# Own buffers for the mirrored gates, and mirror work on 480 of 512 columns in two of three blocks

## The chip, the cores and the metric

The kernel runs on one core of a Trainium2 chip. The metric is the device time of one execution in microseconds (us), given as the median over several executions. The engines are called as in the profile: PE (TensorE matmuls) with PEld (its weight loads), DVE (VectorE), ACT (ScalarE), POOL (GpSimd) and SP (SyncE, which here only issues DMAs). A small q after an engine's name is its instruction queue.

## The reference

The input x has 8 batches of 3008 tokens with 256 features. First comes a Fourier mixing, of which the real part is kept, and then a gated feed-forward layer with 1536 hidden features:

```python
X = np.fft.fft(x, axis=1)
X = np.fft.fft(X, axis=2)
x = X.real.reshape(24064, 256)
gate = np.maximum(x @ w_gate, 0.0)
val = x @ w_val
out = gate * val @ w_out
```

## The kernel before, in words

**Symmetry.** Token k and token 3008 - k of a batch are mirrors: with the feature transform folded into the weights (tiles wc and ws for the cosine and sine parts), both come from the same two rows of numbers P and Q. A token's gate is wc·P + ws·Q, its mirror's is wc·P - ws·Q. The kernel computes the first, reads it, and then adds -2·ws·Q (weights wm) to the same PSUM bank to get the second. The same holds for the value.

**Blocks and steps.** Per batch b there are three blocks of 512 columns (blk 0, 1, 2). A column is a token with its mirror; each group of 32 columns holds the tokens ka + 94·kb of one ka (0 to 47) and all 32 kb. The mirrors of ka = 0 and of ka = 47 lie in the same group, so these two groups are their own mirrors: the first 32 columns of block 0 and the last 32 of block 2. The mirrored half of their results is computed and never stored (`store` leaves it out). Per block there are 12 slices f of 128 hidden features. One step t is one (b, blk, f), 288 in all, and a loop writes the instructions of every engine in the order in which they run (a manual schedule; each engine's queue is in order).

**One step** does the following, with the line numbers of the profile:
- `gate(t)`: two 512-column matmuls into PSUM tile G (L432, L433), and ACT writes the plain gate gs = Relu(G) (L434).
- `mirror_gate(t)`, at the start of step t + 1: one more matmul onto G (L439), and ACT writes the mirrored gate gm = Relu(G) (L442).
- `value(t, 0)`, `value(t, 1)`: two matmuls into V (L449, L451), then DVE writes the plain half of the hidden tile h = gs·V (L453).
- The mirrored value has two forms. A step with t >= 44 and t % 3 != 2 is a *split* step: DVE makes E from V between the two value matmuls (`even`, L459), later E = 2E - V (L473), and POOL multiplies gm·E into the mirrored half of h (`mirror_h`, L465 on POOL). Any other step uses a third value matmul on V (L476), and DVE multiplies gm·V (L465 on DVE).
- `out_piece`: 8 matmuls of 256 columns (L494) for the block 12 steps back, each reading 128 columns of one h tile. Every three steps ACT copies a finished PSUM tile to an output tile os (L497), every six SP issues its four stores (L506 or L512).

So three steps (t % 3 = 0, 1, 2) form a triple with two split steps and one other. In this text a triple runs from one L439 of a step with t % 3 = 0 to the next such one.

**Buffers.** gs and gm share five buffers (pool gp). E has three (ep), os three (op), h 25 (hp). G has two PSUM banks, V three. A buffer is handed on in the order in which its readers stand in the program. In the steady state gs of a step with t % 3 = 0 takes the buffer of gm of step t - 3, and a gs of a step with t % 3 = 1 that of gs of step t - 2.

**The next batch's input.** While batch b is worked on, batch b + 2 is loaded: SP loads xl (L82), POOL issues an indirect load xh (L85). Then POOL folds it (L99 to L108), 22 pieces put one after the other behind the steps' `mirror_h`, from step 13 of each batch for b >= 2 and from step 34 for b = 0 (two per step there). PE's stage 1 (L161, L166) reads the folded tile in the next batch; a shuffle through DRAM (L179, L185), `rotate` (L191) and stage 2 (L203) make the next P and Q. POOL thus has two duties: `mirror_h` for the current step and the fold of a later batch.

Of the kernel before, what the change touches and what calls it, by code (L numbers as in the profile page):

```python
# [11 lines left out]
F32 = mybir.dt.float32  # L12
BF16 = mybir.dt.bfloat16
I32 = mybir.dt.int32
ALU = mybir.AluOpType
ACTF = mybir.ActivationFunctionType
SB = bass.MemoryType.SB
# [9 lines left out]
def free(ap, offset, *dims):  # L27

    part = list(ap.ap[0])
    return bass.AP(ap.tensor, ap.offset + offset, [part] + [list(d) for d in dims])  # L30
# [12 lines left out]
def kernel(ctx: ExitStack, tc, x, w_gate, w_val, w_out, out):  # L43
# [3 lines left out]
    nc = tc.nc  # L47
    B, S, D = x.shape
    DF = w_gate.shape[1]
    NA, NB = 94, 32  # L50
# [3 lines left out]
    NBLK = 3  # L54
# [139 lines left out]
    pqt, nbt = {}, {}  # L194
# [33 lines left out]
    wm = [const.tile([128, DF], BF16, tag=f"wm{i}", name=f"wm{i}") for i in range(2)]  # L228
    wo = const.tile([128, NF, D], BF16, tag="wo")
    af = const.tile([128, NF], F32, tag="af")  # L230
# [38 lines left out]
    with tc.tile_pool(name="sp", bufs=1, space=SB) as sp:  # L269
# [103 lines left out]
        for cs in range(2):  # L373
            t2 = sp.tile([128, 4, NB], F32, tag=f"m2t{cs}")
            nc.vector.tensor_scalar(t2[:], kbi[:], scalar1=mul[:], scalar2=offs[cs][:],
                                    op0=ALU.mult, op1=ALU.add)
# [11 lines left out]
                                op0=ALU.is_equal, op1=ALU.mult)  # L388
# [23 lines left out]
    stage2(0, 0, 1, "dve")  # L412


    gp = ctx.enter_context(tc.tile_pool(name="gp", bufs=5, space=SB))
    ep = ctx.enter_context(tc.tile_pool(name="ep", bufs=3, space=SB))
    op = ctx.enter_context(tc.tile_pool(name="op", bufs=3, space=SB))

    steps = [(b, blk, f) for b in range(B) for blk in range(NBLK) for f in range(NF)]
    ht = {}  # L420

    def split(t):

        return NBLK * NF + 8 <= t < len(steps) and t % 3 != 2

    def gate(t):
        b, blk, f = steps[t]
        pq, fs = pqt[b, blk], slice(f * 128, (f + 1) * 128)
        e = ht[t] = {"h": hp.tile([128, 2, 512], BF16, tag="h", name="h"),
                     "G": psg.tile([128, 512], F32, tag="g", name="G"),  # L430
                     "gs": gp.tile([128, 512], F32, tag="gs", name="gs")}
        nc.tensor.matmul(e["G"][:], lhsT=wc[0][:, fs], rhs=pq[:, 0, :], start=True, stop=False)  # L432
        nc.tensor.matmul(e["G"][:], lhsT=ws[0][:, fs], rhs=pq[:, 1, :], start=False, stop=True)  # L433
        nc.scalar.activation(e["gs"][:], e["G"][:], ACTF.Relu)  # L434

    def mirror_gate(t):
        b, blk, f = steps[t]
        e = ht[t]
        nc.tensor.matmul(e["G"][:], lhsT=wm[0][:, f * 128:(f + 1) * 128], rhs=pqt[b, blk][:, 1, :],  # L439
                         start=False, stop=True, skip_group_check=True)  # L440
        e["gm"] = gp.tile([128, 512], F32, tag="gs", name="gm")
        nc.scalar.activation(e["gm"][:], e["G"][:], ACTF.Relu)  # L442

    def value(t, part):
        b, blk, f = steps[t]
# [8 lines left out]

    def even(t):
        b, blk, f = steps[t]
        e = ht[t]
        e["E"] = ep.tile([128, 512], F32, tag="e", name="E")
        nc.vector.scalar_tensor_tensor(e["E"][:], nbt[b, blk][:], af[:, f:f + 1], e["V"][:],  # L459
                                       op0=ALU.mult, op1=ALU.add)  # L460

    def mirror_h(t, eng, val):

        e = ht[t]
        eng.tensor_tensor(free(e["h"][:], 512 + NB - 1, [NB, 16], [-1, NB]),  # L465
                          e["gm"][:].rearrange("p (a k) -> p a k", k=NB),
                          val[:].rearrange("p (a k) -> p a k", k=NB), op=ALU.mult)

    def mirror_value(t):
        b, blk, f = steps[t]  # L470
        e = ht[t]
        if split(t):
            nc.vector.scalar_tensor_tensor(e["E"][:], e["E"][:], 2.0, e["V"][:], op0=ALU.mult, op1=ALU.subtract)  # L473
            mirror_h(t, nc.gpsimd, e["E"])
        else:
            nc.tensor.matmul(e["V"][:], lhsT=wm[1][:, f * 128:(f + 1) * 128], rhs=pqt[b, blk][:, 1, :],  # L476
                             start=False, stop=True, skip_group_check=True)
            mirror_h(t, nc.vector, e["V"])

# [67 lines left out]
    for t in range(n + NF):  # L547
        if 0 < t <= n:
            mirror_gate(t - 1)
        if t < n:  # L550
            gate(t)
        if 0 < t <= n:
            if split(t - 1):
                value(t - 1, 1)
            else:
                mirror_value(t - 1)
        if t < n and not split(t):
            value(t, 0)
            value(t, 1)
        for fn in extra.get(t, ()):  # L560
            fn()
        if t >= NF:
            out_piece(t - NF, 0)
        if split(t):
            value(t, 0)
            even(t)
        if t >= NF:
            out_piece(t - NF, 1)
        if 0 < t <= n and split(t - 1):
            mirror_value(t - 1)  # L570
        for k in range(2 if t < NBLK * NF + 8 else 1):
            while folds and next(folds[0], folds) is folds:
                folds.pop(0)
# [30 lines left out]
```

## Time and profile before

| | |
|---|---|
| median of 3 runs | 690.17 us (690.15 to 691.46) |
| the profiled execution | 690.58 us, its span 688.8 us |
| granted TensorE clock | 0.998 |
| busy share of the span | PE 95%, PEld 61%, DVE 74%, ACT 63%, POOL 62% |
| first and last gs | 36.6 us and 671.0 us from the span's start |

The profiled execution is 0.41 us above the median; 1.8 us of it lie outside the span. A row of a view of groups gives busy time, mean duration of one instruction in ns, and the idle time of the engine just before these instructions with what ended it. A row of the view of waits gives the waiting instruction, what it waited for, the total in us, the number of times and the longest. A row of the timeline gives start, duration, engine, line and tiles. Matmuls overlap in it: what a matmul costs is the distance to the next start, not its duration.

### The profile page before, as it was taken

The numbers are of one execution on the slowest core, as the hardware profiler recorded it, in microseconds if no ns is written. First come the engines' busy times: TensorE is split into PE (matmuls) and PEld (weight loads), VectorE is DVE, ScalarE is ACT, GpSimd is POOL, SyncE is SP. The second block draws the span as 40 slices with busy tenths as digits, with TensorE's granted clock in tenths as the row PEclk, the third lists the DMA queues.
The fourth block names the chain that finished last, engine by engine and source line by source line (L and its number), as shares of the span: only waits on it lengthen the run. The fifth ranks groups of instructions, "written<-read, shape, count | busy, mean of one in ns | idle before, by whom it ended". The sixth has DMA issues, their size and how long they took to land.

```text
span 688.8 us, 12467 instructions
## 1 busy us (share of the span) xinstructions
PE 653.0 (95%) x4297; PEld 419.5 (61%) x4297; DVE 508.5 (74%) x800; ACT 436.2 (63%) x811; POOL 424.1 (62%) x398
## 2 busy tenths in 40 slices
PE   2799999999999999999999999999899999999996
PEld 1444665666566656666666666666566666666665
DVE  8447555578778778787778878778788788888881
ACT  5555665667676766676666757676666856665561
POOL 1219801984998499747995399846996343344331
PEclk9999999999999999999999999999999999999999
DMA  9692257239314822176112931258211241211213
GB/s 235 216 218 37 63 143 173 48 97 203 113 50 122 199 79 74 40 167 203 38 42 67 234 105 41 74 124 216 59 48 38 60 123 38 78 32 36 54 31 90
DMA packets 31843, 70.74 MB, mean 103 GB/s; under 512 B 4410, under 2 KB 21426, under 8 KB 29394
## 3 DMA queue, kind: packets, MB, share of 16 engines
q1 hardware_dynamic: 29444, 58.16, 31.6%
q0 software_dynamic: 2336, 11.80, 8.4%
q8 instruction: 33, 0.54, 0.4%
q14 instruction: 30, 0.25, 0.1%
HBM read 39.77 MB, written 30.96 MB: 103 GB/s over the span
## 4 chain that ended last, share of the span: by engine, by line
PE 61%; POOL 18%; DMA 10%; issue 5%; DVE 2%; ACT 2%; SPq 1%; POOLq 0%; DVEq 0%
PE po L494 24%; PE V L451 7%; POOL h L465 7%; PE G L439 6%; PE G L432 6%; PE G L433 6%; PE V L449 6%; DMA xl<-in_x_dram 5%; POOL xl L100 4%; POOL xc L99 4%; PE V L476 3%; DMA xh<-in_x_dram,ix 3%; DMA xh<-in_x_dram 2%; PE psw L251 2%; POOL eo L101 2%
## 5 line engine op out<-in xcount | busy, mean ns | idle before, releaser
L494 PE MATMUL po<-wo,h 128*128 128x256 bf16 x2304 | 323.2, 272 | 0.0
L465 POOL TENSOR_TENSOR h<-gm,E 128x512 bf16<-128x512 f32 x162 | 205.9, 1271 | 166.6 <-DVE E L473 166.0
L494 PEld LDWEIGHTS <-h 128*128 128x128 bf16 x2304 | 222.8, 98 | 83.5 <-issue 7.5
L442 ACT ACTIVATE gm<-G 128x512 f32<-128x512 f32 x288 | 172.5, 599 | 129.8 <-PE G L439 128.2
L453 DVE TENSOR_TENSOR h<-gs,V 128x512 bf16<-128x512 f32 x288 | 190.7, 685 | 58.7 <-PE V L451 47.1
L434 ACT ACTIVATE gs<-G 128x512 f32<-128x512 f32 x288 | 171.6, 596 | 15.0 <-POOL h L465 12.6
L465 DVE TENSOR_TENSOR h<-gm,V 128x512 bf16<-128x512 f32 x126 | 86.7, 688 | 85.6 <-ACT gm L442 60.8
L459 DVE SCALAR_TENSOR_TENSOR E<-nb,af,V 128x512 f32<-128x512 bf16 x162 | 120.8, 746 | 6.6 <-PE V L449 6.1
L439 PE MATMUL G<-pq,wm_107 128*128 128x512 bf16 x288 | 109.1, 379 | 9.9 <-ACT gs L434 9.5
L473 DVE SCALAR_TENSOR_TENSOR E<-E,V 128x512 f32<-128x512 f32 x162 | 110.2, 680 | 0.0
L432 PE MATMUL G<-pq,wc_103 128*128 128x512 bf16 x288 | 109.1, 379 | 1.0 <-ACT pq L206 1.0
L449 PE MATMUL V<-pq,wc_104 128*128 128x512 bf16 x288 | 109.1, 379 | 0.0
L433 PE MATMUL G<-pq,ws_105 128*128 128x512 bf16 x288 | 109.1, 379 | 0.0
L451 PE MATMUL V<-pq,ws_106 128*128 128x512 bf16 x288 | 109.0, 379 | 0.0
L497 ACT COPY os<-po 128x512 f32<-128x512 f32 x96 | 56.2, 585 | 67.9 <-PE po L494 67.9
L99 POOL TENSOR_TENSOR xc<-xl,xh 94x768 f32<-94x768 f32 x35 | 63.4, 1811 | 50.0 <-DMA xl<-in_x_dram 34.1
L100 POOL TENSOR_TENSOR xl<-xl,xh 94x768 f32<-94x768 f32 x35 | 63.4, 1812 | 1.6
L433 PEld LDWEIGHTS <-ws_105 128*128 128x128 bf16 x288 | 28.1, 98 | 35.0 <-issue 1.1
L451 PEld LDWEIGHTS <-ws_106 128*128 128x128 bf16 x288 | 28.1, 98 | 34.2 <-DVE ws_106 L256 0.4
L476 PE MATMUL V<-pq,wm_108 128*128 128x512 bf16 x126 | 47.7, 379 | 0.3
L432 PEld LDWEIGHTS <-wc_103 128*128 128x128 bf16 x288 | 28.1, 98 | 18.6 <-issue 15.6
L449 PEld LDWEIGHTS <-wc_104 128*128 128x128 bf16 x288 | 28.2, 98 | 17.6 <-issue 1.3
(361 smaller groups left out, 385.5 us busy)
## 6 DMA issues: line engine op xcount, KB each, us to landing
out_dram<-os SPq DMA_DIRECT2D x176, 128.0 KB
xl<-in_x_dram SPq DMA_DIRECT2D x7, 1360.0 KB
nb<-Nd SPq DMA_DIRECT2D x24, 128.0 KB
xl<-in_x_dram SPq DMA_DIRECT2D x7, 238.0 KB
xl<-in_x_dram SPq DMA_DIRECT2D x2, 768.0 KB
xh<-in_x_dram SPq DMA_DIRECT2D x2, 768.0 KB
wst<-in_moe_w_gate_dram SPq DMA_DIRECT2D x6, 256.0 KB
wst<-in_moe_w_val_dram SPq DMA_DIRECT2D x6, 256.0 KB
```

The source lines that it names most:

```text
L432: nc.tensor.matmul(e["G"][:], lhsT=wc[0][:, fs], rhs=pq[:, 0, :], start=True, stop=False)
L433: nc.tensor.matmul(e["G"][:], lhsT=ws[0][:, fs], rhs=pq[:, 1, :], start=False, stop=True)
L434: nc.scalar.activation(e["gs"][:], e["G"][:], ACTF.Relu)
L439: nc.tensor.matmul(e["G"][:], lhsT=wm[0][:, f * 128:(f + 1) * 128], rhs=pqt[b, blk][:, 1, :], start=False, stop=True, skip_group_check=True)
L442: nc.scalar.activation(e["gm"][:], e["G"][:], ACTF.Relu)
L449: nc.tensor.matmul(e["V"][:], lhsT=wc[1][:, fs], rhs=pq[:, 0, :], start=True, stop=split(t))
L451: nc.tensor.matmul(e["V"][:], lhsT=ws[1][:, fs], rhs=pq[:, 1, :], start=False, stop=True, skip_group_check=split(t))
L453: nc.vector.tensor_tensor(e["h"][:, 0, :], e["gs"][:], e["V"][:], op=ALU.mult)
L459: nc.vector.scalar_tensor_tensor(e["E"][:], nbt[b, blk][:], af[:, f:f + 1], e["V"][:], op0=ALU.mult, op1=ALU.add)
L465: eng.tensor_tensor(free(e["h"][:], 512 + NB - 1, [NB, 16], [-1, NB]), e["gm"][:].rearrange("p (a k) -> p a k", k=NB), val[:].rearrange("p ...
L473: nc.vector.scalar_tensor_tensor(e["E"][:], e["E"][:], 2.0, e["V"][:], op0=ALU.mult, op1=ALU.subtract)
L494: nc.tensor.matmul(po[:, s % 2, :], lhsT=ht[t - f + ff]["h"][:, sg, g * 128:(g + 1) * 128], rhs=wo[:, ff, :], start=(ff == 0), stop=(ff == ...
```

## The change

Three things are changed.

1. gm leaves the pool it shared with gs and gets four buffers of its own, in ep beside E, which goes from three to four. gs keeps two buffers. os goes from three to two. The bytes used are the same. With its own four buffers in turn, gm of step t takes the buffer of gm of step t - 4, and gs that of gs of step t - 2.
2. In blocks 0 and 2 every operation on mirrored gates and values (L439, L442, L459, L465, L473, L476 of before) runs on the 480 columns that have a mirror elsewhere.
3. The 32 columns of h that are left out are set to zero by POOL in `gate` (new line L444), since `out_piece` still reads them. These are 192 memsets, one per step of blocks 0 and 2.

```diff
@@ -412,12 +412,17 @@
     stage2(0, 0, 1, "dve")
 
 
-    gp = ctx.enter_context(tc.tile_pool(name="gp", bufs=5, space=SB))
-    ep = ctx.enter_context(tc.tile_pool(name="ep", bufs=3, space=SB))
-    op = ctx.enter_context(tc.tile_pool(name="op", bufs=3, space=SB))
+    gp = ctx.enter_context(tc.tile_pool(name="gp", bufs=2, space=SB))
+    ep = ctx.enter_context(tc.tile_pool(name="ep", bufs=4, space=SB))
+    op = ctx.enter_context(tc.tile_pool(name="op", bufs=2, space=SB))
 
     steps = [(b, blk, f) for b in range(B) for blk in range(NBLK) for f in range(NF)]
     ht = {}
+
+    def mirrored(t):
+
+        blk = steps[t][1]
+        return slice(NB if blk == 0 else 0, 512 - NB if blk == NBLK - 1 else 512)
 
     def split(t):
 
@@ -432,14 +437,19 @@
         nc.tensor.matmul(e["G"][:], lhsT=wc[0][:, fs], rhs=pq[:, 0, :], start=True, stop=False)
         nc.tensor.matmul(e["G"][:], lhsT=ws[0][:, fs], rhs=pq[:, 1, :], start=False, stop=True)
         nc.scalar.activation(e["gs"][:], e["G"][:], ACTF.Relu)
+        cols = mirrored(t)
+        if cols.stop - cols.start < 512:
+
+            lo = 0 if cols.start else cols.stop
+            nc.gpsimd.memset(e["h"][:, 1, lo:lo + NB], 0.0)
 
     def mirror_gate(t):
         b, blk, f = steps[t]
-        e = ht[t]
-        nc.tensor.matmul(e["G"][:], lhsT=wm[0][:, f * 128:(f + 1) * 128], rhs=pqt[b, blk][:, 1, :],
+        e, cols = ht[t], mirrored(t)
+        nc.tensor.matmul(e["G"][:, cols], lhsT=wm[0][:, f * 128:(f + 1) * 128], rhs=pqt[b, blk][:, 1, cols],
                          start=False, stop=True, skip_group_check=True)
-        e["gm"] = gp.tile([128, 512], F32, tag="gs", name="gm")
-        nc.scalar.activation(e["gm"][:], e["G"][:], ACTF.Relu)
+        e["gm"] = ep.tile([128, 512], F32, tag="gm", name="gm")
+        nc.scalar.activation(e["gm"][:, cols], e["G"][:, cols], ACTF.Relu)
 
     def value(t, part):
         b, blk, f = steps[t]
@@ -454,26 +464,27 @@
 
     def even(t):
         b, blk, f = steps[t]
-        e = ht[t]
+        e, cols = ht[t], mirrored(t)
         e["E"] = ep.tile([128, 512], F32, tag="e", name="E")
-        nc.vector.scalar_tensor_tensor(e["E"][:], nbt[b, blk][:], af[:, f:f + 1], e["V"][:],
+        nc.vector.scalar_tensor_tensor(e["E"][:, cols], nbt[b, blk][:, cols], af[:, f:f + 1], e["V"][:, cols],
                                        op0=ALU.mult, op1=ALU.add)
 
     def mirror_h(t, eng, val):
 
-        e = ht[t]
-        eng.tensor_tensor(free(e["h"][:], 512 + NB - 1, [NB, 16], [-1, NB]),
-                          e["gm"][:].rearrange("p (a k) -> p a k", k=NB),
-                          val[:].rearrange("p (a k) -> p a k", k=NB), op=ALU.mult)
+        e, cols = ht[t], mirrored(t)
+        eng.tensor_tensor(free(e["h"][:], 512 + cols.start + NB - 1, [NB, (cols.stop - cols.start) // NB], [-1, NB]),
+                          e["gm"][:, cols].rearrange("p (a k) -> p a k", k=NB),
+                          val[:, cols].rearrange("p (a k) -> p a k", k=NB), op=ALU.mult)
 
     def mirror_value(t):
         b, blk, f = steps[t]
-        e = ht[t]
+        e, cols = ht[t], mirrored(t)
         if split(t):
-            nc.vector.scalar_tensor_tensor(e["E"][:], e["E"][:], 2.0, e["V"][:], op0=ALU.mult, op1=ALU.subtract)
+            nc.vector.scalar_tensor_tensor(e["E"][:, cols], e["E"][:, cols], 2.0, e["V"][:, cols],
+                                           op0=ALU.mult, op1=ALU.subtract)
             mirror_h(t, nc.gpsimd, e["E"])
         else:
-            nc.tensor.matmul(e["V"][:], lhsT=wm[1][:, f * 128:(f + 1) * 128], rhs=pqt[b, blk][:, 1, :],
+            nc.tensor.matmul(e["V"][:, cols], lhsT=wm[1][:, f * 128:(f + 1) * 128], rhs=pqt[b, blk][:, 1, cols],
                              start=False, stop=True, skip_group_check=True)
             mirror_h(t, nc.vector, e["V"])
```

The order of PE, ACT, DVE and SP is unchanged but for the sizes. POOL's is not. The first place is POOL's queue behind the fold of batch 1, ahead of the load xh for batch 2 (steps 0 to 36). Before:

```order
63 L108 TENSOR_TENSOR eo<-xl 94x2x127 x2
64 L85 DMA xh<-in_x_dram,ix 96x4096
65 L99 TENSOR_TENSOR xc<-xl,xh 94x768
66 L100 TENSOR_TENSOR xl<-xl,xh 94x768
67 L101 TENSOR_TENSOR eo<-xc 94x3x127
```

And with the change, at the same place:

```order
63 L108 TENSOR_TENSOR eo<-xl 94x2x127 x2
64 L444 MEMSET h 128x32 x17
65 L85 DMA xh<-in_x_dram,ix 96x4096
66 L444 MEMSET h 128x32 x6
67 L99 TENSOR_TENSOR xc<-xl,xh 94x768
68 L100 TENSOR_TENSOR xl<-xl,xh 94x768
69 L444 MEMSET h 128x32
70 L101 TENSOR_TENSOR eo<-xc 94x3x127
```

The load xh of batch 2 now stands behind 17 memsets, those of steps 0 to 11 and 24 to 28. The memset of step 28 writes the h buffer of step 3, which `out_piece` reads for the last time at the end of step 22.

The second place is POOL's queue in block 2 of a batch, where `mirror_h` and the fold of a later batch alternate (this piece is in batch 2). Before:

```order
157 L100 TENSOR_TENSOR xl<-xl,xh 94x768
158 L465 TENSOR_TENSOR h<-gm,E 128x16x32
159 L101 TENSOR_TENSOR eo<-xc 94x3x127
160 L103 CAST eo<-xl 94x6
161 L104 TENSOR_TENSOR eo<-xl 94x3x127
162 L465 TENSOR_TENSOR h<-gm,E 128x16x32
163 L99 TENSOR_TENSOR xc<-xl,xh 94x768
164 L465 TENSOR_TENSOR h<-gm,E 128x16x32
```

And with the change:

```order
200 L100 TENSOR_TENSOR xl<-xl,xh 94x768
201 L475 TENSOR_TENSOR h<-gm,E 128x16x32
202 L101 TENSOR_TENSOR eo<-xc 94x3x127
203 L444 MEMSET h 128x32
204 L103 CAST eo<-xl 94x6
205 L104 TENSOR_TENSOR eo<-xl 94x3x127
206 L444 MEMSET h 128x32
207 L475 TENSOR_TENSOR h<-gm,E 128x15x32
208 L99 TENSOR_TENSOR xc<-xl,xh 94x768
209 L444 MEMSET h 128x32
210 L475 TENSOR_TENSOR h<-gm,E 128x15x32
```

Each step of the block puts one memset between the pieces of the fold and the `mirror_h` of the step before, which is one group of 32 columns shorter.

## Prediction

> **What bounds the kernel now.** I read the page first: engine shares and the chain that ended last.
>
> ```profile
> PE 653.0 (95%) x4297; PEld 419.5 (61%) x4297; DVE 508.5 (74%) x800; ACT 436.2 (63%) x811; POOL 424.1 (62%) x398
> PE 61%; POOL 18%; DMA 10%; issue 5%; DVE 2%; ACT 2%; SPq 1%; POOLq 0%; DVEq 0%
> ```
>
> PE is nearly always busy, yet 18% of the chain is POOL, an engine idle 38% of the time: in some stretches POOL holds PE back. The view of waits says how.
>
> ```profile
> ACT gs L434 <- POOL h L465: 12.6, 16, 1.2
> PE G L439 <- ACT gs L434: 9.5, 14, 1.0
> ```
>
> gs takes the buffer in which the gm of three steps earlier lay; that is free when POOL's `mirror_h` has read it, and L439 may not add to G before gs has read G. Asked by stretch of time, the second wait falls nearly all in the four stretches in which POOL folds during batches 2 to 5, about 2.4 us in each; batches 6 and 7, with nothing left to fold, have none. One of them in the timeline (batch 3), with a product of DVE and the gs two steps later:
>
> ```profile
> 322.69 1.27 POOL L465 TENSOR_TENSOR h<-gm,E 128x512 bf16<-128x512 f32 x1
> 324.00 0.60 ACT L434 ACTIVATE gs<-G 128x512 f32<-128x512 f32 x1 [0.91 <-POOL h L465]
> 324.65 0.38 PE L439 MATMUL G<-pq,wm_107 128*128 128x512 bf16 x1 [0.72 <-ACT gs L434]
> 325.78 0.69 DVE L453 TENSOR_TENSOR h<-gs,V 128x512 bf16<-128x512 f32 x1 [1.30 <-PE V L451]
> 327.57 0.59 ACT L434 ACTIVATE gs<-G 128x512 f32<-128x512 f32 x1
> ```
>
> POOL ends at 323.96, gs starts at 324.00, PE 0.72 us late. Outside these stretches PE runs like this (batch 7):
>
> ```profile
> 620.54 0.38 PE L439 MATMUL G<-pq,wm_107 128*128 128x512 bf16 x1
> 621.84 1.04 PE L494 MATMUL po<-wo,h 128*128 128x256 bf16 x8
> 622.71 0.38 PE L439 MATMUL G<-pq,wm_107 128*128 128x512 bf16 x1
> 622.91 0.58 ACT L497 COPY os<-po 128x512 f32<-128x512 f32 x1 [0.81 <-PE po L494]
> 623.39 0.60 ACT L442 ACTIVATE gm<-G 128x512 f32<-128x512 f32 x1
> 624.03 0.69 DVE L465 TENSOR_TENSOR h<-gm,V 128x512 bf16<-128x512 f32 x1 [0.47 <-ACT gm L442]
> 624.63 0.74 DVE L459 SCALAR_TENSOR_TENSOR E<-nb,af,V 128x512 f32<-128x512 bf16 x1
> 625.10 0.38 PE L433 MATMUL G<-pq,ws_105 128*128 128x512 bf16 x1
> 625.43 0.38 PE L451 MATMUL V<-pq,ws_106 128*128 128x512 bf16 x1
> ...
> 626.73 0.38 PE L439 MATMUL G<-pq,wm_107 128*128 128x512 bf16 x1
> ```
>
> The triple takes 6.19 us. Its first step issues six 512-column matmuls from 620.54 to 621.84, 0.216 us each, then eight of 256 columns until 622.71, 0.109 each; 16 and 24 of them need 6.07. The other 0.12 us is L451: it starts 0.33 us after L433, not 0.216, since it overwrites V, which E (L459) reads until 625.37. That is a chain over three engines: the copy of os, gm, h, E, L451.
>
> **Part 1, fewer columns on PE.** 192 steps lie in blocks 0 and 2, and 85 of them use L476 (32 before step 44, 53 after). 256 columns more cost 0.107 us, so 32 columns 13.3 ns: 277 x 13.3 = 3.7 us. All of it is on the path, because PE streams without a gap there.
>
> [...]
>
> **Part 2, the chain in front of L451.** Its pieces shrink as these rows tell:
>
> ```profile
> L442 ACT ACTIVATE gm<-G 128x512 f32<-128x512 f32 x288 | 172.5, 599 | 129.8 <-PE G L439 128.2 <-POOL h L465 1.0 <-DVE h L453 0.5
> L39 ACT ACTIVATE sv<-q 128x128 f32<-128x128 f32 x2 | 0.6, 309 | 2.2 <-DVE q L38 2.2
> L130 DVE TENSOR_TENSOR eo<-xl 94x1016 bf16<-94x1016 f32 x4 | 4.7, 1206 | 0.7 <-DMA xl<-in_x_dram 0.7
> L130 DVE TENSOR_TENSOR eo<-xh 94x889 bf16<-94x889 f32 x1 | 1.1, 1073 | 0.0
> PEld L494 <- issue: 7.5, 32, 0.2
> ```
>
> DVE: 133 ns for 127 elements, so 32 columns are 33 ns, for h and for E. ACT: between 24 ns (290 ns for 384 elements) and 37 (599 in proportion); I take 30. The chain gets 96 ns shorter, PE's own work beside it (two L439, one L476) 40, so the gap falls from 117 to 61 ns: 56 ns a triple beyond part 1. The last row counts weight loads held up behind a late L451, 32 in all. Two thirds of the triples lie in blocks 0 and 2: 21 x 0.056 = 1.2 us (0, if the chain gives nothing, to 3.0, if all 53 split triples there have the gap).
>
> **Part 3, own buffers.** gs no longer waits for POOL; the 9.5 us go. What comes late next is gm(t), behind the `mirror_h` of step t - 4. In POOL's busy stretch this slack shrinks. Its start and end in batch 3, with the gm of step 142 and the `mirror_h` of step 138:
>
> ```profile
> 316.97 1.81 POOL L99 TENSOR_TENSOR xc<-xl,xh 94x768 f32<-94x768 f32 x1 [0.92 <-DMA xh<-in_x_dram,ix]
> 356.63 1.26 POOL L465 TENSOR_TENSOR h<-gm,E 128x512 bf16<-128x512 f32 x1
> ...
> 361.01 0.60 ACT L442 ACTIVATE gm<-G 128x512 f32<-128x512 f32 x1 [0.93 <-PE G L439]
> ```
>
> POOL has no idle time from 316.97 on, so its work decides. gm has 361.01 - 357.89 = 3.1 us. From this go the 2.4 us of waits that vanish ahead of it, about 0.4 for the faster PE (ten steps of 13 to 37 ns), and the memsets, priced by:
>
> ```profile
> L588 POOL MEMSET const-float32-0.0<- 128x1 f32 x1 | 0.1, 98 | 0.3 <-issue 0.3
> L299 POOL MEMSET w_98<- 94x96 bf16 x1 | 0.2, 194 | 0.0
> L298 POOL MEMSET wz<- 94x384 bf16 x1 | 0.4, 434 | 0.0
> L101 POOL TENSOR_TENSOR eo<-xc 94x381 bf16<-94x381 f32 x35 | 34.7, 992 | 0.0
> ```
>
> The two bf16 rows give 0.83 ns a column, so 32 columns are 0.14 us (bounds 0.10 and 0.19, the rows on either side); neighbours on POOL overlap by about 0.05 us (a `mirror_h` of 1.27 us is followed after 1.22), so I charge 0.11. A `mirror_h` has 131 elements more than the last row and takes 0.28 us longer, so 32 columns fewer save 67 ns. By step 142 that is 8 x 0.11 - 5 x 0.067 = 0.5 us. Left: 3.1 - 2.4 - 0.4 - 0.5 = -0.2: gm is 0.2 us late. I take 0.2 us for each of the four stretches: 0.8 us remain. At 0.19 us a memset it is 0.84 each, 3.4 in all; at 0.10 nearly nothing. Part 3 brings 8.7 us (6.1 to 9.5).
>
> One rule prices the memset otherwise. The Trainium skill, GPSIMD Engine Reference, § 3.1, gives a tight loop 1.8 cycles an element at best, 1.2 GHz: 48 ns for 32 columns where the rows show 27. By it each memset costs 0.02 us more, and the sum would be 12.5.
>
> gs, with two buffers, waits for DVE's product of two steps before. In the first timeline it ends at 326.47, 1.1 us ahead of its gs (327.57); part 2 makes DVE earlier, so I charge nothing. os with two buffers: the first copy into a buffer comes three triples, 18.6 us, after its last store was issued, and 512 KB need 3.3 us at the 160 GB/s of a window below: nothing.
>
> **Part 4, what is moved.** xh of batch 2 goes from 82.93 us to behind step 22:
>
> ```profile
> 82.93 1.00 POOL L85 DMA_INDIRECT xh<-in_x_dram,ix  x1 [0.15 <-issue]
> 90.92 1.04 PE L494 MATMUL po<-wo,h 128*128 128x256 bf16 x8
> 92.00:95.00 3.00, 3.00 (x20) 1.89 (x19) 1.33 (x3) 2.29 (x5) 0.00 (x0) 1.00 0.00 0
> 95.00:103.00 8.00, 8.00 (x57) 5.29 (x56) 4.29 (x7) 5.78 (x11) 0.00 (x0) 1.00 0.56 160
> 118.08 1.80 POOL L99 TENSOR_TENSOR xc<-xl,xh 94x768 f32<-94x768 f32 x1 [34.15 <-DMA xl<-in_x_dram]
> 148.56 1.28 POOL L465 TENSOR_TENSOR h<-gm,E 128x512 bf16<-128x512 f32 x1 [0.45 <-ACT gm L442]
> 154.52 0.60 ACT L442 ACTIVATE gm<-G 128x512 f32<-128x512 f32 x1 [0.68 <-PE G L439]
> ```
>
> It starts at 92 us. Its 96 x 16 KB = 1.57 MB find room up to 103 us (the last column is GB/s; I count 220, near the page's highest slices): 0.6 MB by 95, 0.5 by 103. The remaining 0.5 MB push the shuffle and xl by 2.4 us at most. `rotate` waits for no DMA in before; how early the shuffle lands for it no row shows. The fold of batch 2 starts at 120.5 instead of 118.08 and holds 12 memsets more (1.3 us), so the first `mirror_h` ends at 153.5 instead of 149.84, and the gm that needs its buffer stands at 154.52 minus about 1.0 already won (32 steps by two matmuls, 0.85, and a few split ones): just in time. I charge 0.4 us (0 to 3, if the delay passes through to PE here or at the next `rotate`). The 17 memsets ahead of xh hold up nobody else: stage 1 of batch 1 needs only the fold before them, and `out_piece` reads these columns from 91.4 us on, 8 us after the fold's end.
>
> **The sum.** 3.7 + 1.2 + 8.7 - 0.4 = 13.2 us off the profiled 690.58, 677.4; the profile stands 0.41 above the median, so 690.17 - 13.2 = 677.0. Bounds of this case: 3.7 + 3.0 + 9.5 = 16.2 gives 674.0; 3.7 + 0 + 6.1 - 3 = 6.8 gives 683.4.
>
> **Rivals.**
> - *The wait only moves (0.10).* If POOL's throughput is the limit of the busy stretches, gm waits there for `mirror_h` instead of gs, the 9.5 us stay and only parts 1 and 2 remain: 690.17 - 4.9 = 685.3. For it: POOL is full from 316.97 to the end of the stretch. Against it: the slack of 3.1 us at its end, and POOL idle right afterwards.
> - *The memsets hold POOL too long (0.05), slower.* Place: the four busy stretches. Past 0.11 us each extra 0.1 us on a memset puts 0.8 us on a stretch, 3.2 us in all, since PE there follows POOL. The 13.2 us are used up when a memset occupies POOL 0.52 us; at 0.7 us it would be 690.17 - 13.2 + 18.9 = 695.9. Against it: no memset row above 0.43 us, and that for twelve times the columns.
> - *gs now waits for DVE (0.05), no change.* Two gs buffers bind if the product comes over 1.1 us later. At 0.16 us a triple over the 81 split triples the gain is gone: 690.2. For it: DVE is the second busiest engine; against it: it starts that product as soon as L451 lets it.
>
> That the change does less than it says is no rival: the order has all 192 memsets and the 480 columns.
>
> **The numbers.** The forecast has 0.80. Its bounds reach from 674.0 to 683.4; sizes may be off beyond that, so the range goes on to the first rival: 674.0 to 685.3. About 0.2% (1.4 us) is what a measurement can tell here. Faster by more: forecast and first rival, 0.90; within: third rival, 0.05; slower: second rival, 0.05.
>
> **What would show it.** Right: no wait of gs for POOL and none of L439 for gs above a microsecond in total; 480-column matmuls followed 0.20 us later; triples of batch 7 of 6.08 us in blocks 0 and 2 and 6.19 in block 1; memsets near 0.14 us; xh of batch 2 at 92 us. Wrong: gm or L439 waiting for POOL's h for several us, memsets over 0.3 us, gs waiting for DVE's h, or `rotate` waiting for the shuffle.

## The result and the profile after

The changed kernel takes 675.32 us (median of 4 runs, 675.09 to 675.36), the kernel before in the same session 690.48 us. The ratio is 0.9777, with a 95% interval of 0.976 to 0.979. The profiled execution is 675.27 us, its span 673.5 us at a granted clock of 0.998. So 15.2 us are gone where 13.2 were forecast.

The engines' shares and the chain that ended last, from the page of after:

```profile
PE 643.4 (96%) x4218; PEld 419.9 (62%) x4297; DVE 500.8 (74%) x800; ACT 428.9 (64%) x811; POOL 428.5 (64%) x590
PE 94%; DMA 2%; DVE 2%; issue 1%; ACT 1%; SPq 0%; DVEq 0%; ACTq 0%
```

POOL is a little busier than before (428.5 us against 424.1) and yet gone from the chain that ended last, in which it had 18%. The groups of the two waiting instructions, and what is left in the view of waits of gm behind POOL:

```profile
L439 ACT ACTIVATE gs<-G 128x512 f32<-128x512 f32 x288 | 171.8, 597 | 2.2 <-POOL si L399 2.2
L449 PE MATMUL G<-pq,wm_107 128*128 128x480 bf16 (+1 forms) x288 | 106.7, 371 | 1.0 <-ACT gs L439 1.0
ACT gm L452 <- POOL xc L99: 1.9, 2, 0.9
ACT gm L452 <- POOL h L475: 1.0, 1, 1.0
ACT gm L452 <- POOL h L444: 0.7, 1, 0.7
```

gs (now L439) waits for POOL once, at the start, for a tile of the prologue. The mirrored matmul (now L449) waits 1.0 us in all, once, in batch 0. The last three rows name POOL as what came last, but it held up no gm: in these four steps gm starts 0.46 to 0.48 us after its L449, as elsewhere (median 0.46 for t % 3 = 1), and the `mirror_h` that frees its buffer had ended at least 1.15 us before. A triple of batch 7, block 0, in the timeline, starting at the same one of the three steps as the triple in the prediction (the rows of L449 at its start, one step later and at its end, and the chain):

```profile
599.67 0.37 PE L449 MATMUL G<-pq,wm_107 128*128 128x480 bf16 x1
601.83 0.37 PE L449 MATMUL G<-pq,wm_107 128*128 128x480 bf16 x1
602.03 0.59 ACT L508 COPY os<-po 128x512 f32<-128x512 f32 x1 [0.83 <-PE po L505]
602.51 0.58 ACT L452 ACTIVATE gm<-G 128x480 f32<-128x480 f32 x1
603.12 0.65 DVE L475 TENSOR_TENSOR h<-gm,V 128x480 bf16<-128x480 f32 x1 [0.48 <-ACT gm L452]
603.69 0.71 DVE L469 SCALAR_TENSOR_TENSOR E<-nb,af,V 128x480 f32<-128x480 bf16 x1
604.17 0.38 PE L438 MATMUL G<-pq,ws_105 128*128 128x512 bf16 x1
604.45 0.38 PE L461 MATMUL V<-pq,ws_106 128*128 128x512 bf16 x1
605.75 0.37 PE L449 MATMUL G<-pq,wm_107 128*128 128x480 bf16 x1
```

The triple takes 6.08 us instead of 6.19. The chain of os copy, gm, h and E is still there: E ends at 604.40 and L461 starts at 604.45, 0.28 us after L438 instead of 0.216. Its gap has shrunk from 117 to about 60 ns.

POOL during the fold in batch 3 (where step 142 stands, as in the prediction), with the gm of that step:

```profile
349.34 0.13 POOL L444 MEMSET h<- 128x32 bf16 x1
349.49 1.81 POOL L100 TENSOR_TENSOR xl<-xl,xh 94x768 f32<-94x768 f32 x1
351.24 0.13 POOL L444 MEMSET h<- 128x32 bf16 x1
351.31 1.21 POOL L475 TENSOR_TENSOR h<-gm,E 128x480 bf16<-128x480 f32 x1
352.91 0.57 ACT L452 ACTIVATE gm<-G 128x480 f32<-128x480 f32 x1 [0.94 <-PE G L449]
```

`mirror_h` of step 138 ends at 352.52, 0.39 us ahead of the gm that takes its buffer. The same slack stands at step 106 in batch 2; the least in the kernel is 0.20 us, at step 214 in batch 5. A memset's row is 0.13 us, but the instruction behind it starts 0.07 us after the memset's start at 351.24 (0.15 at 349.34, in front of an L100).

**How runs are compared below.** The first mirrored matmul comes at 37.0 to 39.3 us, differently in each trace, and no edit changes the prologue in front of it. So next to the whole time stands the *loop*, from the start of the first mirrored matmul to that of the last (288 of them, none missing in these traces), and its parts. Each row is one traced execution. Worked out from those starts, in us:

```text
                       batches  batches 2-5                  batches
                       0, 1     block 0  block 1  block 2    6, 7      loop
before                 168.04   104.81   107.03   105.89     149.24    635.01
after                  166.30   103.03   100.90   101.40     147.95    619.58
own buffers            167.65   104.30   100.89   102.55     149.39    624.78
480 columns            167.35   103.65   107.30   105.99     147.79    632.07
gm 3 buffers           166.30   102.84   101.53   106.47     147.90    625.04
PE on 512              167.26   103.56   100.89   102.04     148.36    622.11
8 spare memsets        171.97   108.69   101.47   118.06     148.52    648.70
late copy              165.97   103.10    99.53   106.06     146.77    621.42
late copy, early load  165.98   102.72    99.53   100.85     146.58    615.66
late copy, gm 6        165.97   102.54    99.53   100.79     146.47    615.29
and later tables       163.11   102.54    99.53   100.79     146.47    612.44
```

The loop got 15.4 us shorter, 10.6 of them in blocks 1 and 2 of batches 2 to 5, where POOL folds.

### The profile page after: what moved, and what is told of

The parts are those of the page before. It is cut to its first block, busy times and chain, and to the rows that moved or that the text cites. A ratio compares the mean times of both kernels' runs of the same rounds, so it can differ in the third digit from the quotient of the medians.

```text
span 673.5 us, 12515 instructions
## 1 busy us (share of the span) xinstructions
PE 643.4 (96%) x4218; PEld 419.9 (62%) x4297; DVE 500.8 (74%) x800; ACT 428.9 (64%) x811; POOL 428.5 (64%) x590
## 4 chain that ended last, share of the span: by engine, by line
PE 94%; DMA 2%; DVE 2%; issue 1%; ACT 1%; SPq 0%; DVEq 0%; ACTq 0%
PE po L505 38%; PE G L438 10%; PE V L461 9%; PE G L449 9%; PE V L459 8%; PE G L437 8%; PE V L487 4%; PE psw L251 4%; DMA xh<-in_x_dram 2%; DVE h L463 1%; DVE eo L130 0%; DVE E L469 0%; SPq L119 0%; ACT gm L452 0%; ACT os L508 0%
## 5 line engine op out<-in xcount | busy, mean ns | idle before, releaser
L475 POOL TENSOR_TENSOR h<-gm,E 128x480 bf16<-128x480 f32 (+1 forms) x162 | 199.1, 1229 | 147.9 <-DVE E L483 147.2
L452 ACT ACTIVATE gm<-G 128x480 f32<-128x480 f32 (+1 forms) x288 | 167.4, 581 | 134.0 <-PE G L449 130.4
L439 ACT ACTIVATE gs<-G 128x512 f32<-128x512 f32 x288 | 171.8, 597 | 2.2 <-POOL si L399 2.2
L475 DVE TENSOR_TENSOR h<-gm,V 128x480 bf16<-128x480 f32 (+1 forms) x126 | 83.7, 664 | 87.8 <-ACT gm L452 63.2
L469 DVE SCALAR_TENSOR_TENSOR E<-nb,af,V 128x480 f32<-128x480 bf16 (+1 forms) x162 | 117.2, 723 | 7.4 <-PE V L459 5.9
L438 PE MATMUL G<-pq,ws_105 128*128 128x512 bf16 x287 | 108.8, 379 | 2.0
L449 PE MATMUL G<-pq,wm_107 128*128 128x480 bf16 (+1 forms) x288 | 106.7, 371 | 1.0 <-ACT gs L439 1.0
L483 DVE SCALAR_TENSOR_TENSOR E<-E,V 128x480 f32<-128x480 f32 (+1 forms) x162 | 106.6, 658 | 0.0
L461 PE MATMUL V<-pq,ws_106 128*128 128x512 bf16 x272 | 103.0, 379 | 0.2
L459 PE MATMUL V<-pq,wc_104 128*128 128x512 bf16 x265 | 100.5, 379 | 0.0
L437 PE MATMUL G<-pq,wc_103 128*128 128x512 bf16 x249 | 94.4, 379 | 1.0 <-ACT pq L206 1.0
L100 POOL TENSOR_TENSOR xl<-xl,xh 94x768 f32<-94x768 f32 x35 | 63.5, 1814 | 1.2
L461 PEld LDWEIGHTS <-ws_106 128*128 128x128 bf16 x288 | 28.2, 98 | 33.8 <-DVE ws_106 L256 0.4
L438 PEld LDWEIGHTS <-ws_105 128*128 128x128 bf16 x288 | 28.2, 98 | 32.4 <-issue 1.1
L487 PE MATMUL V<-pq,wm_108 128*128 128x480 bf16 (+1 forms) x126 | 46.6, 370 | 0.2
L459 PEld LDWEIGHTS <-wc_104 128*128 128x128 bf16 x288 | 28.2, 98 | 17.5 <-issue 1.3
L104 POOL TENSOR_TENSOR eo<-xl 94x381 bf16<-94x381 f32 x35 | 34.8, 995 | 0.0
```

Source lines behind the costliest of these rows:

```text
L449: nc.tensor.matmul(e["G"][:, cols], lhsT=wm[0][:, f * 128:(f + 1) * 128], rhs=pqt[b, blk][:, 1, cols], start=False, stop=True, skip_group_ ...
L452: nc.scalar.activation(e["gm"][:, cols], e["G"][:, cols], ACTF.Relu)
L459: nc.tensor.matmul(e["V"][:], lhsT=wc[1][:, fs], rhs=pq[:, 0, :], start=True, stop=split(t))
L461: nc.tensor.matmul(e["V"][:], lhsT=ws[1][:, fs], rhs=pq[:, 1, :], start=False, stop=True, skip_group_check=split(t))
L469: nc.vector.scalar_tensor_tensor(e["E"][:, cols], nbt[b, blk][:, cols], af[:, f:f + 1], e["V"][:, cols], op0=ALU.mult, op1=ALU.add)
L475: eng.tensor_tensor(free(e["h"][:], 512 + cols.start + NB - 1, [NB, (cols.stop - cols.start) // NB], [-1, NB]), e["gm"][:, cols].rearrange ...
```

## The experiments

The theory is that of the prediction: POOL's late `mirror_h` held PE through the shared buffers, and own buffers of sufficient depth end that; the columns are worth what PE and the chain in front of L461 save. The rivals are that the wait only moves to gm, that the memsets decide, and that PE had room for the columns anyway.

**Own buffers alone.** All operations stay on 512 columns, so there is no memset.

```diff
     def mirrored(t):
-        blk = steps[t][1]
-        return slice(NB if blk == 0 else 0, 512 - NB if blk == NBLK - 1 else 512)
+        return slice(0, 512)
```

> Own buffers alone (gm 4, E 4, gs 2, os 2); all mirror work on 512 columns in every block, no memsets. Theory: the waits of gs for POOL's h are the cost of the shared buffers, so about 9.5 to 10 us go without any trimmed column: about 680.5 us (680.0 to 682.0), no wait of PE for gs in the four fold stretches. Rival 1: POOL's throughput limits those stretches, the wait only moves to gm: about 690 us, with gm waiting for POOL's h for some 9 us. Rival 2: the buffers help only together with the shorter work: between 684 and 690 us.

Measured: 682.27 us, ratio 0.9863 (0.9846 to 0.988); the loop is 10.2 us shorter. The group of gs, and the chain, of this kernel:

```profile
L439 ACT ACTIVATE gs<-G 128x512 f32<-128x512 f32 x288 | 171.5, 595 | 3.1 <-POOL si L399 3.1
PE 92%; issue 2%; DMA 2%; DVE 2%; POOL 1%; ACT 0%; SPq 0%; DVEq 0%; ACTq 0%; POOLq 0%
```

gs waits for POOL only at the start, for the tile of the prologue. 6.1 us come from block 1 and 3.3 us from block 2 of batches 2 to 5. E and os have their new depths here too, and neither was changed alone. The trace of before speaks against a part of theirs: no E starts there less than 2.47 us after the product that frees its buffer, and os waits for PE alone.

**480 columns alone,** with the pools of before.

```diff
-    gp = ctx.enter_context(tc.tile_pool(name="gp", bufs=2, space=SB))
-    ep = ctx.enter_context(tc.tile_pool(name="ep", bufs=4, space=SB))
-    op = ctx.enter_context(tc.tile_pool(name="op", bufs=2, space=SB))
+    gp = ctx.enter_context(tc.tile_pool(name="gp", bufs=5, space=SB))
+    ep = ctx.enter_context(tc.tile_pool(name="ep", bufs=3, space=SB))
+    op = ctx.enter_context(tc.tile_pool(name="op", bufs=3, space=SB))
...
-        e["gm"] = ep.tile([128, 512], F32, tag="gm", name="gm")
+        e["gm"] = gp.tile([128, 512], F32, tag="gs", name="gm")
```

> 480 columns and memsets alone, with the pools of before (gs and gm share five buffers, E three, os three). Theory: parts 1 and 2 are worth about 5.4 us by the blocks without waits, and the waits of gs for POOL stay at 9 to 10 us, since a memset costs POOL about as much as the shorter product saves: about 685 us (684 to 687). Rival: the shorter work on POOL clears the stretches by itself: below 680 us.

Measured: 688.43 us (9 runs), ratio 0.9959 (0.9945 to 0.9972), a smaller gain than expected; the loop is 2.9 us shorter. Given own buffers, the same columns are worth 624.78 - 619.58 = 5.2 us. The view of waits of this kernel tells where the rest stayed:

```profile
PE G L449 <- ACT gs L439: 12.4, 20, 1.0
ACT gs L439 <- POOL h L475: 14.2, 17, 1.2
```

PE's wait for gs was 9.5 us before. While POOL sets the pace, a faster PE waits longer: blocks 2 of batches 2 to 5, in which every mirrored matmul is shorter, gain nothing (105.99 us against 105.89). So the two halves of the change are not independent, and 2.3 us exist only with both.

**Three buffers for gm instead of four.**

```diff
-        e["gm"] = ep.tile([128, 512], F32, tag="gm", name="gm")
+        e["gm"] = ep.tile([128, 512], F32, tag="gm", bufs=3, name="gm")
```

> The changed kernel with three buffers for gm instead of four, nothing else. Theory: the gm of a split step then waits for the product of step t - 3, one step (about 2 us) less slack; the smallest slacks of 0.2 to 0.6 us become about -1.6 us, of which PE feels 1.1 to 1.6 us in each of the four stretches: 679.5 to 682 us. Rival: leaving the shared pool is what counts, three do as well: 675.3 us.

Measured: 681.09 us, ratio 0.985 (0.9836 to 0.9864); the loop is 5.5 us longer than in after. Waits of this kernel:

```profile
ACT gm L452 <- POOL h L475: 25.5, 22, 1.5
PE G L449 <- ACT gs L439: 4.7, 10, 1.0
```

gm waits for POOL, gs stands behind gm on ACT, PE behind gs: the first rival's mechanism. The four blocks 2 lose 5.1 us. So not the separation of gm as such, but its depth decides, and four is just enough.

**The mirrored matmuls back on 512 columns,** all else on 480.

```diff
-        nc.tensor.matmul(e["G"][:, cols], lhsT=wm[0][:, f * 128:(f + 1) * 128], rhs=pqt[b, blk][:, 1, cols],
+        nc.tensor.matmul(e["G"][:], lhsT=wm[0][:, f * 128:(f + 1) * 128], rhs=pqt[b, blk][:, 1, :],
...
-            nc.tensor.matmul(e["V"][:, cols], lhsT=wm[1][:, f * 128:(f + 1) * 128], rhs=pqt[b, blk][:, 1, cols],
+            nc.tensor.matmul(e["V"][:], lhsT=wm[1][:, f * 128:(f + 1) * 128], rhs=pqt[b, blk][:, 1, :],
```

> The changed kernel with the mirrored matmuls back on 512 columns; ACT, DVE and POOL stay on 480. Theory (columns count where PE streams, and part of them disappears in the gap where the chain decides): 2.4 to 2.8 us more than 619.6 us between the first and the last mirrored matmul. Columns alone, without the chain: 3.7 us more. If PE had room, as its share of weight loads would say: no change.

Measured: 678.88 us, ratio 0.9821 (0.9804 to 0.9838); the loop is 2.5 us longer than in after. PE therefore had no room to spare, but the columns are not worth 3.7 us once the rest is done. A triple of batch 7 in this kernel:

```profile
606.15 0.38 PE L449 MATMUL G<-pq,wm 128*128 128x512 bf16 x1
606.58 0.38 PE L438 MATMUL G<-pq,ws 128*128 128x512 bf16 x1
606.82 0.38 PE L461 MATMUL V<-pq,ws 128*128 128x512 bf16 x1
612.24 0.38 PE L449 MATMUL G<-pq,wm 128*128 128x512 bf16 x1
```

It takes 6.09 us against 6.08 with 480 columns. In a triple like this one the chain in front of L461 decides, and PE's shorter matmuls are given back as a longer gap there: L461 starts 0.24 us after L438 here and 0.28 with 480 columns. The columns count in the triples that have no such gap.

**Dearer memsets.** First, every memset was issued eight times into the same columns.

```diff
-            nc.gpsimd.memset(e["h"][:, 1, lo:lo + NB], 0.0)
+            for k in range(8):
+                nc.gpsimd.memset(e["h"][:, 1, lo:lo + NB], 0.0)
```

> The changed kernel with every memset issued eight times (each eats about 0.057 us more of POOL, so a step's zeroing goes from 0.07 to about 0.45 us). Theory: POOL's slack at the end of a fold stretch is some 0.4 us plus 0.5 us that PE has in hand, the extra work there is 8 x 0.4 = 3.2 us, so PE waits about 2.5 us in each of the four stretches and 3 to 5 us around the folds of batches 2 and 3: 687 to 693 us. Rival: POOL is idle for a third of the span, the memsets are hidden: 675 to 676 us.

Measured: 778.21 us, ratio 1.126 (1.123 to 1.129), far beyond the expectation. The group of the memsets, and the chain, of this kernel:

```profile
L445 POOL MEMSET h<- 128x32 bf16 x1536 | 187.3, 124 | 77.5
POOL 44%; PE 36%; issue 8%; DMA 6%; DVE 3%; ACT 1%; SPq 0%; POOLq 0%; DVEq 0%; ACTq 0%
```

With the idle time in front of them they take (187.3 + 77.5) / 1536 = 0.17 us each, since each now starts only after the end of the one before it. That is 1.4 us a step, and POOL became the bound. As a price for one memset it is useless; so the eight were put into eight different places of a tile that nobody reads:

```diff
+    spare = ctx.enter_context(tc.tile_pool(name="spare", bufs=1, space=SB)).tile([128, 8, NB], BF16, tag="spare", name="spare")
...
             nc.gpsimd.memset(e["h"][:, 1, lo:lo + NB], 0.0)
+            for k in range(8):
+                nc.gpsimd.memset(spare[:, k, :], 0.0)
```

> The changed kernel with eight more memsets a step, each into a place of its own in a spare tile, so that none waits for the one before (those of the run with eight into the same columns did: 0.17 us each). At 0.06 us each a step's zeroing takes about 0.55 us of POOL instead of 0.07. Theory of the slack: 8 x 0.48 = 3.8 us by the step with the least slack, of which 0.4 is free and 0.5 in hand, so 2.9 us of waiting in each of four stretches, and 2 to 5 us in the folds of batches 2 and 3: 15 to 21 us more between the first and the last mirrored matmul than the changed kernel's 619.6 us. Rival: POOL's idle third hides them: no change.

Measured: 703.87 us, ratio 1.0196 (1.0166 to 1.0226): slower than before the change. The loop is 29.1 us longer than in after, also more than expected. POOL and the wait of gm in this kernel:

```profile
300.79 0.14 POOL L445 MEMSET h<- 128x32 bf16 x1
300.85 0.56 POOL L447 MEMSET spare<- 128x32 bf16 x8
301.33 0.14 POOL L445 MEMSET h<- 128x32 bf16 x1
ACT gm L455 <- POOL h L478: 59.3, 37, 5.2
```

A memset that waits for none occupies POOL for 0.06 us, eight for 0.48 us. Each 0.1 us more a step costs about 29.1 / 4.8 = 6.1 us, nearly twice the 3.2 us that the second rival reckoned. The table shows why. Blocks 2 of batches 2 to 5 lose 16.7 us, which is about 8.7 steps each, as reckoned; but another 5.7 us each are lost in batches 0 and 1 and in blocks 0 of batches 2 to 5, where POOL also folds or is still behind from a fold, and which the rival left out.

**The chain in front of L461 cut.** ACT's copy of os, and the stores behind it, are put behind the gm and gs of the next step.

```diff
-                nc.scalar.copy(os_[:, s - 1:s + 1, :], po[:])
+                late.append(lambda os_=os_, po=po, s=s: nc.scalar.copy(os_[:, s - 1:s + 1, :], po[:]))
...
-                store(b, blk, sg, os_)
+                late.append(lambda a=(b, blk, sg, os_): store(*a))
...
         if t < n:
             gate(t)
+        flush()
```

> The changed kernel with ACT's copy into os put behind gm and gs of the next step instead of ahead of them. Theory: the gap in front of the first value matmul of every third step (0.12 us in block 1, 0.06 in half of the triples of blocks 0 and 2) comes from the chain os copy, gm, DVE's h, E; without the copy at its head it closes: 3 to 5 us less than 619.6 us between the first and the last mirrored matmul, triples of batch 7 of 6.02 and 6.07 us. Rival: the gap is PE's own (writing V that DVE has just read): no change. Rival: gs or G is held up by the copy instead: slower.

Measured: 676.52 us, ratio 0.979 (0.9767 to 0.9812), no gain over after, against expectation; the loop is 1.8 us longer. The chain is cut as meant: triples of batch 7 take 6.02 us in block 0 (one of four 6.13) and 6.07 in block 1 (6.08 and 6.19 in after), which is the time of their matmuls alone, and blocks 1 of batches 2 to 5 are 1.4 us shorter in all. But blocks 2 there are 4.7 us longer. In the view of waits gm now stands behind POOL:

```profile
ACT gm L452 <- POOL h L475: 53.4, 47, 1.9
```

The start of the fold in batch 2 on POOL, with the `mirror_h` in front of it. In after:

```profile
233.25 1.27 POOL L475 TENSOR_TENSOR h<-gm,E 128x512 bf16<-128x512 f32 x1 [3.83 <-DVE E L483]
235.20 1.81 POOL L99 TENSOR_TENSOR xc<-xl,xh 94x768 f32<-94x768 f32 x1 [0.68 <-DMA xh<-in_x_dram,ix]
```

With the late copy:

```profile
232.19 1.27 POOL L475 TENSOR_TENSOR h<-gm,E 128x512 bf16<-128x512 f32 x1 [3.83 <-DVE E L483]
235.84 1.81 POOL L99 TENSOR_TENSOR xc<-xl,xh 94x768 f32<-94x768 f32 x1 [2.38 <-DMA xh<-in_x_dram,ix]
```

PE and with it `mirror_h` are 1.1 us earlier on the clock (0.6 of it because the loop starts earlier in this trace), but xh lands no earlier. POOL stands at the fold's first instruction for 2.38 us instead of 0.68, with the next steps' `mirror_h` queued behind it, and the 0.39 us of slack are used up: in 34 steps of this kernel gm starts within 0.06 us of the end of the `mirror_h` that frees its buffer, in after in none.

In batches 3 to 5 POOL waits there 1.94 to 2.31 us for xl, and not for xh. The load of xl in batch 3, in after:

```profile
293.05 0.83 SPq L82 DMA_DIRECT2D xl<-in_x_dram  x2
```

With the late copy, and the start of the fold behind it:

```profile
294.31 0.85 SPq L82 DMA_DIRECT2D xl<-in_x_dram  x2
312.96 1.81 POOL L99 TENSOR_TENSOR xc<-xl,xh 94x768 f32<-94x768 f32 x1 [2.08 <-DMA xl<-in_x_dram]
```

SP issues this load 0.47 us after the L449 of step 114 in after and 1.69 us after it with the late copy. On SP's queue it stands behind four stores, and these now wait for the later copy (their first is issued at 292.50 instead of 291.25 us). So the late copy itself moves the load, and with it the fold, back against the steps.

Two readings of the loss were left: the fold's late start through gm's four buffers, or po and os, which the late copy frees later. Two edits tell them apart. Six buffers for gm:

```diff
-        e["gm"] = ep.tile([128, 512], F32, tag="gm", name="gm")
+        e["gm"] = ep.tile([128, 512], F32, tag="gm", bufs=6, name="gm")
```

> The late copy with six gm buffers in place of four. Theory: the late copy's gain was handed back in the four blocks 2 of batches 2 to 5 (26.41 to 26.72 us there against 25.35 in the changed kernel), because gm found its buffer still held by a POOL that had started the fold late. With six buffers gm looks back six steps and does not meet POOL: those four blocks take 25.2 to 25.4 us, the loop 621.43 - 4.5 = about 617, the kernel about 672. Rival: the late copy itself slows these blocks (copy and store later, so po or os later): they stay at 26.4 us or more and the loop at 621.

Or the loads two steps earlier (in batches 1 to 5, not 1 to 3 as the expectation has it):

```diff
-            1: (12, 19, range(11, 19), 19, 26, (26, 27, 29, 31, 33, 35)),
-            2: (7, 13, range(6, 14), 14, 22, (23, 25, 27, 29, 31, 33))}
+            1: (10, 19, range(11, 19), 19, 26, (26, 27, 29, 31, 33, 35)),
+            2: (5, 13, range(6, 14), 14, 22, (23, 25, 27, 29, 31, 33))}
```

> The late copy with four gm buffers as before, but the loads of the tokens issued two steps (about 4 us) earlier in batches 1 to 3. Theory: POOL's fold began 1 to 2 us late in the block because its first instruction stood waiting for xh, with the mirrored products queued behind it; two steps earlier the load has landed when POOL gets there, the wait of the fold for DMA is gone in batches 3 to 5, and the blocks 2 fall back to 25.2 to 25.5 us: loop about 617 to 618. Rival: POOL's throughput over the whole fold is the limit, not its start: then an earlier fold only moves the wait to an earlier step and the blocks stay over 26 us.

Measured: 671.63 us, ratio 0.9714 (0.9695 to 0.9732), with six buffers, and 672.77 us, 0.9739 (0.9713 to 0.9765), with earlier loads. In both, blocks 2 of batches 2 to 5 fall to 100.8 us. With the earlier loads two rows of gm behind POOL remain, 35.8 us in all:

```profile
ACT gm L452 <- POOL h L444: 20.0, 18, 1.4
ACT gm L452 <- POOL h L475: 15.8, 15, 1.3
```

They are nearly all no waits for a buffer: only in steps 106 and 107 does gm start right behind its `mirror_h` (0.03 us), in the others that had ended at least 1.26 us before. With six buffers it ends at least 1.77 us ahead of gm. So the loss went through the fold's start and gm's four buffers, not through po or os. The late copy had a part in it, since it put the load of xl back.

**Everything that helped, together.** Two waits of PE are left inside the loop of after. Stage 2 (L203) waits there for the tile t that `rotate` writes (L192):

```profile
PE ps_1264 L203 <- DVE t_1073 L192: 1.4, 1, 1.4
PE ps_2153 L203 <- DVE t_1949 L192: 1.1, 1, 1.1
```

They went when the first stage-2 pieces of batches 0 and 1 came one step later, here on top of the late copy:

```diff
-    plan = {0: (28, 34, (14, 16, 18, 19, 21, 23, 24, 25), 26, 33, (33, 34, 36, 38, 40, 42)),
-            1: (12, 19, range(11, 19), 19, 26, (26, 27, 29, 31, 33, 35)),
+    plan = {0: (28, 34, (14, 16, 18, 19, 21, 23, 24, 25), 26, 33, (34, 35, 36, 38, 40, 42)),
+            1: (12, 19, range(11, 19), 19, 26, (27, 28, 29, 31, 33, 35)),
```

> The late copy, and stage 2 of batches 1 and 2 one step later, so that PE does not stand still for DVE's copy between rotate and stage 2 (1.4 and 1.1 us of waits in the changed kernel's profile, both in one step with rotate). Theory: the gain of the late copy plus 2.5 us: 613 to 615 us between the first and the last mirrored matmul, about 668 to 671 us in all. Rival: the later stage 2 makes the next batch's first step wait: 0 to 2 us of the 2.5.

Measured: 674.55 us, ratio 0.9759 (0.9735 to 0.9783). The two blocks with those waits are 1.6 and 1.3 us shorter than with the late copy alone; the long blocks 2 remain. Then with six buffers for gm and the earlier loads as well:

> Late copy, the tables for batch 1 one step later, earlier loads and six gm buffers together. If the gains add, the loop is 616.5 - 2.8 (the two waits for the tables) = about 613.5 to 615 and the kernel 670 to 671.5; if POOL's throughput is a limit of its own, not under 617 and 673.

Measured: 670.95 us, ratio 0.9697 (0.9676 to 0.9717); the loop is 614.0 us. One step in batch 2, block 1, takes 3.55 us instead of 1.95. ACT and the queue of SP in this kernel:

```profile
235.85 0.59 ACT L513 COPY os<-po 128x512 f32<-128x512 f32 x1 [2.38 <-DMA out_dram<-os]
SPq L82 <- POOL h L444: 23.3, 3, 12.3
```

The earlier load stands on SP's queue waiting for POOL to be done with xl, stores stand behind it (issued from 217.44 us on), and the os buffer that they hold comes free late. With earlier loads and four gm buffers the same order cost a wait of 0.59 us at that copy and no step grew longer. So the last kernel is the same without the earlier loads:

> The kernel with late copy, later tables and six gm buffers, but the loads of the tokens at their old steps. In the version with earlier loads one step of block 7 took 3.55 us instead of 1.95: a copy of os there waited 2.38 us for the stores of its buffer, which had stood on SP's queue behind a load that waited 12.3 us for POOL. Theory: the earlier load causes this wait; without it block 7 takes 24.88 us again, the other blocks stay as they are, and the loop is 614.03 - 1.6 = 612.4 (kernel about 669). Rival: the later tables or the late copy cause it: block 7 stays at 26.5 and the loop at 614.

Measured: 668.59 us (668.45 to 672.05), ratio 0.9686 (0.9661 to 0.9712), with a loop of 612.4 us as expected. The wait needed the earlier load. This is the fastest version: 1% below the changed kernel by the two ratios, whose intervals do not meet.

A version that zeroes each h buffer's columns once, and not at every step, was not tried. What the memsets still cost in the changed kernel stays open.

## Why the prediction was right, and where its sizes were off

**What bounds the kernel** was read rightly: with own buffers alone the waits of gs for POOL are gone, and so are 10.2 us.

**Parts 1 and 2** were 4.9 us together; the runs give 5.2 (after against own buffers alone). The 61 ns forecast for the gap in front of L461 are there: a triple of batch 7, block 0, takes 6.08 us with the gap and, with the late copy, 6.02 without it. What the split into two parts does not say is that they overlap: where the chain decides, the matmuls' columns give 0.01 us a triple, and taken back alone they cost 2.5 us of the 3.7. PE's weight loads, 61% of the span before and 62% after, must not be read as room on PE: with all else on 480 columns, mirrored matmuls of 512 columns cost 2.5 us. The Trainium skill (Perfetto Trace Analysis, § Identifying the Most-Contended Engine) sets matmul busy time aside and judges TensorE by MFU, the share of its peak that the matmuls use, together with the share of weight loads. Here the weight loads alone would mislead. An estimate of how full PE is, from the starts in before, agrees with the run: 1566 matmuls of 512 columns at 0.216 us and 2304 of 256 columns at 0.109 us fill 589 of the 688.8 us, 86%.

**Part 3** is the term that was mis-sized: 10.2 us (own buffers alone) against 8.7. Of the difference, 0.8 is the lateness of gm that was charged and did not come. At step 142 the slack is +0.39 us, not -0.2. With own buffers alone it is 0.89 us there, where the terms of the prediction give 3.1 - 2.4 = 0.7; that is 0.2 of the 0.6. The rest is about what the memset was charged too much: 0.11 us against 0.06, over eight memsets 0.4 us. (From an L104 to the `mirror_h` behind it are 0.95 us with own buffers alone, and 1.01 us in after with a memset between the two.)

The other 0.7 us is the difference between the 9.5 us that were expected to go and the 10.2 that went, and here two errors partly cancel, which is luck. The 9.5 us were the whole wait of L439 for gs. One of its pieces has no POOL behind it:

```profile
61.00 0.38 PE L439 MATMUL G<-pq,wm_107 128*128 128x512 bf16 x1 [0.96 <-ACT gs L434]
```

In front of this gs ACT had stood 2.16 us at a weight tile (L257), and the wait is still there in after, the 1.0 us of L449. So about 8.4 us of waits inside the loop lay behind POOL (1.4 to 2.3 us in each of the four stretches, not 2.4), and the loop lost 1.8 us more than these. About two thirds of that is in blocks 2 of batches 2 to 5, where 2.1 us of such waits were and 3.3 us were saved. What the 1.8 us are was not followed; that cause stays open.

**Part 4** was charged 0.4 us and cost nothing. The rows that decide it, of after:

```profile
92.83 1.01 POOL L85 DMA_INDIRECT xh<-in_x_dram,ix  x1 [0.64 <-PE V L487]
119.18 1.81 POOL L99 TENSOR_TENSOR xc<-xl,xh 94x768 f32<-94x768 f32 x1 [24.80 <-DMA xl<-in_x_dram]
153.80 0.60 ACT L452 ACTIVATE gm<-G 128x512 f32<-128x512 f32 x1 [0.68 <-PE G L449]
```

The load is issued at 92.83 as forecast, but the fold starts 1.1 us later than before, not 2.4. The first `mirror_h` behind the fold ends at 151.08, not 153.5, and its gm comes 2.7 us after that.

**The rivals.** The first has its mechanism and not its place: it decides at three buffers, and again at four once the fold starts later against the steps, as with the late copy: 1.7 us in batch 2 (0.64 us later on the clock, with the steps 1.06 us earlier) and 1.4 in batch 3. The second is real and nearer than reckoned: at 6.1 us for each 0.1 us, the gain of 15.4 is used up when a memset occupies POOL 0.25 us longer, at about 0.31 us and not 0.52 (an estimate on a straight line between two kernels). The third did not come: gs never waits for DVE, whose product ends at least 1.00 us ahead of it.

## What to carry to other kernels

A ring of buffers shared by a fast and a slow reader lets the slow one stop the fast one's writer; look at who frees the buffer, and count how many steps back its last reader may be. When such a wait is removed, measure the slack that is left: here it was 0.20 to 0.55 us in the four stretches, and the next improvement was lost to it until the ring got deeper or the slow engine began earlier. A row of the view of waits that names POOL is not yet a delay; compare the end of the last reader with the start of the writer. And before moving a load or a store in a queue, name what will stand behind it while it waits.

## What the runs showed that was not expected

- A small memset's row is longer than what it occupies: 0.126 us in the rows of after, 0.06 us to the next start. When each writes what the one before has written, it is 0.17 us.
- Between kernels that differ only in the loop, the loop's first mirrored matmul comes anywhere from 37.0 to 39.3 us. This 2.3 us lies in front of every edit and is larger than several of the effects. The loop alone is far steadier: blocks 1 of batches 2 to 5 take 99.53 us in each of the four kernels with the late copy in the table.
